# Moving the scaling of expert sums to the scalar engine, and issuing a group's token combinations closer together

## The chip, the cores and the metric

The kernel runs on one core of a Trainium2 chip. The metric is device time in microseconds (us) of one execution; lower is better. The engines are named as in the profile: PE is the TensorE matrix engine (PEld its weight loads), DVE the VectorE, ACT the ScalarE, POOL the GpSimd engine, SP the SyncE that issues most of the DMAs.

## The reference

The part that the change touches is the second half of the reference. `x` is the output of an attention stage, reordered to 2304 tokens of 512 features. `P` is a 2304 x 8 matrix of expert weights that eight rounds of row and column normalisation (Sinkhorn) make out of a softmax numerator.

```python
    logits = x @ w_gate
    P = np.exp(logits - logits.max())
    for _ in range(8):
        P /= P.sum(1, keepdims=True) + 1e-09
        P /= P.sum(0, keepdims=True) + 1e-09
        P *= N / E
    out = np.zeros((N, D), dtype=np.float32)
    for e in range(E):                       # 8 experts, every token goes through each
        h = np.maximum(x @ w1[e], 0.0)       # 512 -> 1024
        ye = h @ w2[e]                       # 1024 -> 512
        out += P[:, e:e + 1] * ye
```

## The kernel before

The attention stage fills the first 280 us or so and leaves `x` in SBUF as a high and a low part (`xh`, `xl`). Every matmul operand is split in this way, since PE multiplies rounded operands: a high part is a cast on ACT, the low part a subtraction of the high part from the full value, on POOL or DVE, and each product is three matmuls (high by high, high by low, low by high).

The expert stage works on three groups `g` of 768 tokens (6 tiles of 128, index `j`). Within a group it goes through `ITEMS`: a pair of an expert `e` and a quarter `part` of its 1024 hidden features. The first quarter of expert 0 is computed for all tokens ahead of the expert stage and stored in DRAM (`ydr`), so a group has 31 items and there are 93 in all, numbered `q` here from 0. In turn `q` the kernel computes

- the first products of item `q` (x by w1, then ReLU and the split of the result into `hhh` and `hhl`), and
- the second products of item `q - 1` (`second`, lines 868 to 884): for each `j`, six matmuls of 512 columns into one of three PSUM banks (`py`), and a DVE instruction that adds the result to the running sum `acc[:, j]`.

Most items are "fast": `first_fast` computes the first products with seven block products in place of eight by sums and differences of blocks, a Strassen-Winograd scheme (`p1, p6, p2, p7, p4, p5, p3` in this order). It needs four combinations of token blocks per group, `tcomb` (a high part `th` and a low part `tl`, index 0 to 3), which `t_tasks(g)` makes out of `xh` and `xl` in the scratch buffers `temps`. A few items are "plain" (eight block products in four pieces): items 0 to 3, and the last two of groups 0 and 1 (29, 30, 60, 61). While these run, `temps` and `tcomb` are free, and the combinations of the next group are made; the first fast item after them (4, 31 and 62) uses them from its second product on. So a fast turn has 13 pieces (7 first, 6 second), a plain one 10.

The weights of item `q + 1` are split during turn `q`: `w1_split` and `w2_split` hand out a list of jobs, one of which is issued behind each piece; casts go to ACT (`w1h`, L750 and L755, `w2h`, L778), subtractions to POOL (`w1l`, L751 and L756, `w2l`, L779).

The orders of ACT and DVE are those in which the code issues the instructions (`tc.manual_schedule`). The orders of PE, POOL and SP are set by the framework's planner when the kernel is built. Each engine runs its own list in order, with semaphores between engines.

Two things of this stage are changed. One is the scaling with expert 0's weight. For expert 0 the sums are added without a weight (L874); when expert 1 begins, ahead of the first weighted sum of each tile, DVE multiplies the running sum by expert 0's weight `P[:, t_, 0:1]` (L877), in turns 4, 35 and 66. From then on the sum is one instruction that multiplies by the weight and adds (L878). The other is the pace of `t_tasks`: twelve tasks, one in each of those pieces whose count modulo 8 is 0, 3 or 6, and one in every piece once as many tasks are left as pieces. A task `split` issues an ACT cast to `th` (L713) and the subtraction to `tl` (L710), on POOL for three of the four and on DVE for the last. The router's eight rounds (`rows`, `colmat`, `colsum`, L576 to L597) run on DVE and PE in the same turns 0 to 3 as group 0's combinations, four pieces to a round; `colmat` is a matmul into the tile `cp` that waits for `rows`.

At the end of a group the sums are stored to the output (L884) and the next group's start values are loaded from `ydr` (`acc_load`, L888), both on the queue of SP.

Of the kernel before, what the change touches and what calls it, by code (L numbers as in the profile page):

```python
# [17 lines left out]
def kernel(  # L18
# [13 lines left out]
    nc = tc.nc  # L32
# [44 lines left out]
    P = const.tile([128, NTILE, E], F32, name="P")  # L77
# [19 lines left out]
    def f32(ap):  # L97
        return ap.bitcast(F32)
# [533 lines left out]
    def product2(pt, hh, hl, w2h, w2l, cols):  # L632
        n = 0
        for f in range(2):
            for h_, w in ((hh, w2h), (hh, w2l), (hl, w2h)):
                nc.tensor.matmul(  # L636
                    out=pt, lhsT=h_[:, f, cols], rhs=w[:, f], start=(n == 0), stop=(n == 5)
                )
                n += 1
# [23 lines left out]
    HT = 384  # L663
    NG = NT // (2 * HT)

    def experts():
# [11 lines left out]
        acc = mp.tile([128, 2 * HT // 128, DM], F32, name="acc")  # L678
        tasks = router_tasks()
        tasks.reverse()  # L680

        def tick():
            if tasks:
                tasks.pop()()

        ITEMS = [
            (g, e, part) for g in range(NG) for e in range(E) for part in range(NQ)
            if (e, part) != (0, 0)
        ]
        per = E * NQ - 1  # L690
        plain = set(range(4)) | {g * per - j for g in range(1, NG) for j in (1, 2)}


        def blk(x, g, kh, th):
            c0 = (2 * g + th) * HT
            return x[:, 2 * kh:2 * kh + 2, c0:c0 + HT]

        def t_tasks(g):
            th, tl = tcomb
            s0, s1, s2 = (temps[:, i] for i in range(3))  # L700
            d, p_ = nc.vector, nc.gpsimd

            def full(o, kh, t2, eng):
                eng.tensor_tensor(
                    out=o.rearrange("p (k c) -> p k c", k=2), in0=f32(blk(xh, g, kh, t2)),
                    in1=f32(blk(xl, g, kh, t2)), op=ALU.add,
                )

            def sub(o, x, y, eng):
                eng.tensor_tensor(out=o, in0=x, in1=y, op=ALU.subtract)  # L710

            def split(i, src, eng):
                nc.scalar.copy(out=th[:, i], in_=src)  # L713
                sub(tl[:, i], src, f32(th[:, i]), eng)

            return [
                lambda: full(s0, 0, 1, d), lambda: full(s1, 0, 0, d), lambda: full(s2, 1, 1, p_),
                lambda: sub(s1, s0, s1, d), lambda: split(0, s1, p_), lambda: sub(s0, s2, s0, d),
                lambda: split(2, s0, p_), lambda: sub(s2, s2, s1, d), lambda: full(s0, 1, 0, d),
                lambda: split(1, s2, p_), lambda: sub(s0, s0, s2, d), lambda: split(3, s0, d),  # L720
            ]

        def w1_load(q):
            g, e, part = ITEMS[q]
            pool = mq if q % 2 else mp
            raws = [pool.tile([128, 512], F32, tag="raw", name="raw", bufs=2) for _ in range(2)]
            for j, raw in enumerate(raws):
                nc.sync.dma_start(
                    out=raw.rearrange("p (k f) -> p k f", k=2),
                    in_=w1[e, 256 * j:256 * j + 256, part * FQ:part * FQ + FQ]  # L730
                    .rearrange("(k p) f -> p k f", p=128),
                )
            return raws
# [9 lines left out]
        def w1_split(q, raws):  # L743
            wh, wl = w1s[q % 2]
            r0, r1 = (r.rearrange("p (k f c) -> p k f c", k=2, f=2) for r in raws)
            a11, a21, a12, a22 = r0[:, :, 0], r0[:, :, 1], r1[:, :, 0], r1[:, :, 1]
            tt = nc.gpsimd.tensor_tensor

            def one(i, src):
                nc.scalar.copy(out=wh[:, i], in_=src)  # L750
                tt(out=wl[:, i], in0=src, in1=f32(wh[:, i]), op=ALU.subtract)  # L751

            def two(i, raw):
                src = raw.rearrange("p k f c -> p f k c")
                nc.scalar.copy(out=wh[:, i:i + 2], in_=src)  # L755
                tt(out=wl[:, i:i + 2], in0=src, in1=f32(wh[:, i:i + 2]), op=ALU.subtract)  # L756


            def comb_a():
                tt(out=a22, in0=a21, in1=a22, op=ALU.add)  # L760
                tt(out=a21, in0=a11, in1=a21, op=ALU.subtract)

            def comb_b():
                tt(out=a11, in0=a22, in1=a11, op=ALU.subtract)
                tt(out=a12, in0=a12, in1=a11, op=ALU.subtract)

            if q in plain:
                return [lambda: two(1, r1), lambda: one(0, a11), lambda: one(3, a21)]
            return [
                lambda: two(1, r1), lambda: one(0, a11), comb_a, comb_b,  # L770
                lambda: two(3, r0), lambda: two(5, r1),
            ]

        def w2_split(q, raws):
            wh, wl = w2s[(q + 1) % 2]

            def one(j):
                nc.scalar.copy(out=wh[:, j], in_=raws[j])  # L778
                nc.gpsimd.tensor_tensor(  # L779
                    out=wl[:, j], in0=raws[j], in1=f32(wh[:, j]), op=ALU.subtract  # L780
                )

            return [lambda: one(0), lambda: one(1)]
# [84 lines left out]
        def second(q, j):  # L868
            g, e, part = ITEMS[q]
            t_ = 2 * HT // 128 * g + j  # L870
            pt = py[j % 3]
            product2(pt, *hs[q % 2], *w2s[(q + 1) % 2], slice(128 * j, 128 * j + 128))
            if e == 0:
                nc.vector.tensor_tensor(out=acc[:, j], in0=pt, in1=acc[:, j], op=ALU.add)  # L874
            else:
                if (e, part) == (1, 0):
                    nc.vector.tensor_scalar_mul(acc[:, j], acc[:, j], P[:, t_, 0:1])  # L877
                nc.vector.scalar_tensor_tensor(  # L878
                    out=acc[:, j], in0=pt, scalar=P[:, t_, e:e + 1], in1=acc[:, j],
                    op0=ALU.mult, op1=ALU.add,  # L880
                )
            if q % per == per - 1:
                eng = nc.scalar if g == NG - 1 and j % 2 else nc.sync
                eng.dma_start(out=out[128 * t_:128 * t_ + 128, :], in_=acc[:, j])  # L884

        def acc_load(g):
            for j in range(2 * HT // 128):
                nc.sync.dma_start(out=acc[:, j], in_=ydr[2 * HT // 128 * g + j])  # L888
# [16 lines left out]
        todo = t_tasks(0)  # L905
# [4 lines left out]
        steps, left, late = [0], [34], []  # L910
        with tc.manual_schedule(engines={mybir.EngineType.Activation, mybir.EngineType.DVE}):
            for q in range(NI + 1):
                jobs = []
                if q < NI:
                    back = w2_split(q, r2.pop(q))
                if q + 1 < NI:
                    if q + 2 < NI:
                        r1[q + 2] = w1_load(q + 2)
                    jobs = w1_split(q + 1, r1.pop(q + 1))
                    back.append(lambda q=q: r2.__setitem__(q + 1, w2_load(q + 1)))  # L920
                    jobs[4:4] = back + [lambda: None]
                elif q < NI:
                    jobs = back
                if q in plain and q + 1 in plain and q > 4:
                    todo += t_tasks(q // per + 1)
                    left[0] = 20
                pieces = (first_plain if q in plain else first_fast)(q) if q < NI else []
                if q:
                    pieces += [lambda j=j: second(q - 1, j) for j in range(2 * HT // 128)]
                for f in pieces:  # L930
                    n = len(late)
                    f()
                    for _ in range(n):
                        late.pop(0)()
                    tick()
                    if jobs:
                        jobs.pop(0)()
                    steps[0] += 1
                    if todo and (steps[0] % 8 in (0, 3, 6) or len(todo) >= left[0]):
                        todo.pop(0)()  # L940
                    left[0] -= 1
                for f in jobs:
                    f()
                if q < NI and q and q % per == 0:
                    acc_load(q // per)

    setup()
    attention()
    front.close()
    experts()  # L950


# [28 lines left out]
```

## Time and profile before

| what | value |
|---|---|
| time, three runs | 1772.06, 1772.59, 1774.39 us; median 1772.59 |
| span of the profiled execution, first to last instruction | 1770.6 us (no separate time is listed for it) |
| PE busy | 1723.7 us, 97% |
| DVE busy | 1289.0 us, 73% |
| ACT busy | 685.7 us, 39% |
| POOL busy | 1166.0 us, 66% |
| granted TensorE clock, mean | 0.996 |

A busy time is a mean over all stages; the rows further down are of single stretches. "Chain" is the chain of work that ended last, followed back from the last instruction. Matmuls overlap, so the duration of one in the trace is longer than the distance between two starts.

### The profile page before, as it was taken

How to read it: one execution, taken by the hardware profiler on the slowest of the kernel's cores; microseconds unless marked ns; L12 is line 12 of the kernel's file. 1: busy time of each engine (PE TensorE's matmuls, PEld its weight loads, DVE VectorE, ACT ScalarE, POOL GpSimd, SP SyncE). 2: the span in 40 equal slices, each digit the busy share in tenths (PEclk: the TensorE clock that was granted, in tenths of full speed). 3: DMA queues.
4: the chain of work that ended last, by engine and by line, in shares of the span. 5: the costliest groups of instructions: out<-in, count | busy, mean ns of one | idle time of the engine just before them, and what ended most of it. 6: DMA issues, size and time to landing. Idle time of an engine off the chain costs nothing.

```text
span 1770.6 us, 26969 instructions
## 1 busy us (share of the span) xinstructions
PE 1723.7 (97%) x9381; PEld 1522.5 (86%) x9381; DVE 1289.0 (73%) x2371; ACT 685.7 (39%) x1550; POOL 1166.0 (66%) x1113
## 2 busy tenths in 40 slices
PE   5899999999999999999999999999999999999999
PEld 4677777889999999888899999998898999999998
DVE  6887873787777777767777777777667777777776
ACT  4766762233333333333333333333333333333332
POOL 4655543567777777676677777776676777777773
PEclk8999999999999999999999999999999999999999
DMA  4443414222222222214222222222142222222221
GB/s 109 105 103 96 114 41 149 57 70 71 72 66 61 65 72 72 72 49 142 72 71 61 65 66 72 72 72 72 48 143 72 65 61 66 72 72 72 72 60 48
DMA packets 154888, 135.55 MB, mean 77 GB/s; under 512 B 71424, under 2 KB 121728, under 8 KB 154752
## 3 DMA queue, kind: packets, MB, share of 16 engines
q1 hardware_dynamic: 154320, 133.05, 25.0%
q8 instruction: 74, 1.21, 0.3%
q10 hardware_dynamic: 432, 0.79, 0.1%
q14 instruction: 62, 0.51, 0.1%
HBM read 124.28 MB, written 9.51 MB: 76 GB/s over the span
## 4 chain that ended last, share of the span: by engine, by line
PE 81%; POOL 5%; DVE 4%; issue 4%; DMA 2%; ACT 2%; SPq 1%; POOLq 0%; ACTq 0%; DVEq 0%
PE s L636 40%; PE s L805 27%; PE f L805 9%; PE x L470 1%; ACT e L324 1%; DMA rsb<-rd 1%; PE s L303 1%; DVE hhl L790 1%; POOL tl L710 1%; POOL phi L425 1%; POOL w1l L756 1%; DVE acc L877 0%; PE s L621 0%; PE f L636 0%; POOL w2l L779 0%
## 5 line engine op out<-in xcount | busy, mean ns | idle before, releaser
L756 POOL TENSOR_TENSOR w1l<-raw,w1h 128x512 fp32r<-128x512 f32 x263 | 368.2, 1414 | 395.1 <-ACT w1h L755 394.9
L878 DVE SCALAR_TENSOR_TENSOR acc<-s,P,acc 128x512 f32<-128x512 f32 x504 | 369.2, 745 | 133.5 <-PE s L636 131.1
L636 PE MATMUL s<-w2h,hhh 128*128 128x512 f32 x1116 | 435.5, 390 | 6.0 <-DVE acc L878 5.9
L636 PE MATMUL s<-w2h,hhl 128*128 128x512 f32 x1116 | 436.1, 391 | 0.0
L636 PE MATMUL s<-w2l,hhh 128*128 128x512 f32 x1116 | 435.8, 391 | 0.0
L836 DVE TENSOR_TENSOR temps<-s,temps 128x384 f32<-128x384 f32 x447 | 242.5, 555 | 169.8 <-ACT w1h L755 83.0
L790 DVE SCALAR_TENSOR_TENSOR hhl<-temps,hhh 128x384 fp32r<-128x384 f32 x340 | 306.5, 901 | 0.0
L779 POOL TENSOR_TENSOR w2l<-raw,w2h 128x512 fp32r<-128x512 f32 x186 | 292.7, 1595 | 11.9 <-ACT w2h L778 11.9
L789 ACT ACTIVATE hhh<-temps 128x384 fp32r<-128x384 f32 x340 | 178.7, 526 | 297.8 <-DVE temps L836 289.9
L636 PEld LDWEIGHTS s<-w2h,hhh 128*128 128x128 f32 x1116 | 209.6, 188 | 50.6 <-DVE acc L878 9.5
L636 PEld LDWEIGHTS s<-w2h,hhl 128*128 128x128 f32 x1116 | 209.4, 188 | 44.0
L636 PEld LDWEIGHTS s<-w2l,hhh 128*128 128x128 f32 x1116 | 209.4, 188 | 41.5
L839 ACT COPY temps<-s 128x384 f32<-128x384 f32 x64 | 30.7, 480 | 413.7 <-PE s L805 412.6
L805 PE MATMUL s<-th,w1l 128*128 128x384 f32 x510 | 170.8, 335 | 1.5 <-POOL w1l L756 1.5
L805 PE MATMUL s<-tl,w1h 128*128 128x384 f32 x510 | 170.7, 335 | 0.8 <-POOL tl L710 0.8
L805 PE MATMUL s<-th,w1h 128*128 128x384 f32 x510 | 170.6, 334 | 0.0
L805 PE MATMUL s<-xh,w1l 128*128 128x384 f32 x480 | 161.7, 337 | 0.5 <-POOL w1l L751 0.5
L805 PE MATMUL s<-xh,w1h 128*128 128x384 f32 x480 | 161.7, 337 | 0.0
L805 PE MATMUL s<-xl,w1h 128*128 128x384 f32 x480 | 161.2, 336 | 0.0
L755 ACT CAST w1h<-raw 128x512 fp32r<-128x512 f32 x263 | 153.7, 615 | 3.7 <-issue 3.0
L836 DVE TENSOR_TENSOR temps<-f,temps 128x384 f32<-128x384 f32 x148 | 80.3, 555 | 55.3 <-PE f L805 26.2
L778 ACT CAST w2h<-raw 128x512 fp32r<-128x512 f32 x186 | 112.1, 607 | 0.0
(220 smaller groups left out, 2895.0 us busy)
## 6 DMA issues: line engine op xcount, KB each, us to landing
raw<-in_moe_w_dram SPq DMA_DIRECT2D x372, 256.0 KB
rsb<-rd SPq DMA_DIRECT2D x32, 144.0 KB
ydr<-wst SPq DMA_DIRECT2D x18, 256.0 KB
acc<-ydr SPq DMA_DIRECT2D x18, 256.0 KB
qraw<-in_q_dram SPq DMA_DIRECT2D x32, 128.0 KB
kraw<-in_k_dram SPq DMA_DIRECT2D x32, 128.0 KB
vraw<-in_v_dram SPq DMA_DIRECT2D x32, 128.0 KB
out_dram<-acc SPq DMA_DIRECT2D x15, 256.0 KB
```

What stands on the lines that cost most here:

```text
L303: nc.tensor.matmul(out=sp[h][:, at:at + w], lhsT=qq[x][half[h], 128 * i:128 * i + 128], rhs=kk[y][half[h], 0:w], start=(a == 0), stop=(a = ...
L636: nc.tensor.matmul(out=pt, lhsT=h_[:, f, cols], rhs=w[:, f], start=(n == 0), stop=(n == 5))
L755: nc.scalar.copy(out=wh[:, i:i + 2], in_=src)
L756: tt(out=wl[:, i:i + 2], in0=src, in1=f32(wh[:, i:i + 2]), op=ALU.subtract)
L778: nc.scalar.copy(out=wh[:, j], in_=raws[j])
L779: nc.gpsimd.tensor_tensor(out=wl[:, j], in0=raws[j], in1=f32(wh[:, j]), op=ALU.subtract)
L789: nc.scalar.activation(out=hh[:, f, c], in_=src, func=AF.Relu)
L790: late.append(lambda: nc.vector.scalar_tensor_tensor(out=hl[:, f, c], in0=src, scalar=0.0, in1=f32(hh[:, f, c]), op0=ALU.max, op1=ALU.subt ...
L805: nc.tensor.matmul(out=pt[:, 0:HT], lhsT=w[:, wi, k], rhs=x[:, k], start=(n == 0), stop=(n == total - 1),)
L836: nc.vector.tensor_tensor(out=o, in0=x, in1=y, op=ALU.add)
L839: nc.scalar.copy(out=X, in_=prod(q, [(0, b11)]))
L878: nc.vector.scalar_tensor_tensor(out=acc[:, j], in0=pt, scalar=P[:, t_, e:e + 1], in1=acc[:, j], op0=ALU.mult, op1=ALU.add,)
```

## The change

Three edits, all in the expert stage. First, the multiplication by expert 0's weight becomes an ACT instruction (`acc_scale`), issued two pieces ahead of the sum that uses it; in group 0 in turn 4 as before, in groups 1 and 2 directly after the start values are loaded, in turns 32 and 63. Second, since in groups 1 and 2 the start values are now scaled ahead of expert 0's own items, these use the weighted sum (36 sums). Third, `t_tasks` becomes a list of eleven steps, some with two instructions; for groups 1 and 2 the piece count starts at 0 with the first plain turn and a step is issued in three pieces of four; the low parts 2 and 1 move from POOL to DVE, so that only low part 0 is on POOL.

```diff
+        scaled = [(0, 1, 0)] + [(g, 0, 1) for g in range(1, NG)]
...
-            def split(i, src, eng):
+            def hi(i, src):
                 nc.scalar.copy(out=th[:, i], in_=src)
+
+            def lo(i, src, eng):
                 sub(tl[:, i], src, f32(th[:, i]), eng)

             return [
-                lambda: full(s0, 0, 1, d), lambda: full(s1, 0, 0, d), lambda: full(s2, 1, 1, p_),
-                lambda: sub(s1, s0, s1, d), lambda: split(0, s1, p_), lambda: sub(s0, s2, s0, d),
-                lambda: split(2, s0, p_), lambda: sub(s2, s2, s1, d), lambda: full(s0, 1, 0, d),
-                lambda: split(1, s2, p_), lambda: sub(s0, s0, s2, d), lambda: split(3, s0, d),
+                [lambda: full(s0, 0, 1, d)],
+                [lambda: full(s1, 0, 0, d), lambda: full(s2, 1, 1, p_)],
+                [lambda: sub(s1, s0, s1, d)],
+                [lambda: sub(s0, s2, s0, d), lambda: hi(2, s0)],
+                [lambda: sub(s2, s2, s1, d), lambda: hi(1, s2)],
+                [lambda: lo(2, s0, d), lambda: hi(0, s1)],
+                [lambda: lo(1, s2, d)],
+                [lambda: full(s0, 1, 0, d), lambda: lo(0, s1, p_)],
+                [lambda: sub(s0, s0, s2, d), lambda: hi(3, s0)],
+                [lambda: None],
+                [lambda: lo(3, s0, d)],
             ]
...
-            if e == 0:
+            if e == 0 and g == 0:
                 nc.vector.tensor_tensor(out=acc[:, j], in0=pt, in1=acc[:, j], op=ALU.add)
             else:
-                if (e, part) == (1, 0):
-                    nc.vector.tensor_scalar_mul(acc[:, j], acc[:, j], P[:, t_, 0:1])
                 nc.vector.scalar_tensor_tensor(
...
+        def acc_scale(g, j):
+            t_ = 2 * HT // 128 * g + j
+            nc.scalar.mul(acc[:, j], acc[:, j], P[:, t_, 0:1])
...
                     todo += t_tasks(q // per + 1)
                     left[0] = 20
+                    steps[0] = 0
...
+                scales = []
+                if q and ITEMS[q - 1] in scaled:
+                    scales = [None] * (len(pieces) - 2 * HT // 128 - 2) + [
+                        lambda j=j: acc_scale(ITEMS[q - 1][0], j) for j in range(2 * HT // 128)
+                    ]
                 for f in pieces:
+                    if scales:
+                        s_ = scales.pop(0)
+                        if s_:
+                            s_()
...
-                    if todo and (steps[0] % 8 in (0, 3, 6) or len(todo) >= left[0]):
-                        todo.pop(0)()
+                    pace = steps[0] % 4 != 3 if q > 4 else steps[0] % 8 in (0, 3, 6)
+                    if todo and (pace or len(todo) >= left[0]):
+                        for t_ in todo.pop(0):
+                            t_()
```

## Rows read from the trace of the kernel before

**Rows 1.** The page's head: span and instructions.

```profile
span 1770.6 us, 26969 instructions
```

**Rows 2.** Chain, in order of time: start us, us, what; turns 4, 31, 35, 62 to 67.

```profile
358.89 3.14 PE s L805 x18
...
371.44 1.46 DVE acc L877
...
377.17 1.06 PE f L805 x6
...
802.91 1.06 PE s L805 x6
...
849.43 1.06 PE f L805 x6
...
867.38 1.06 PE s L805 x6
...
1291.09 2.10 PE s L805 x12
...
1298.40 8.20 PE s L636 x36
...
1313.90 8.20 PE s L636 x36
...
1337.61 1.06 PE s L805 x6
...
1355.61 2.10 PE s L805 x12
```

**Rows 3.** Timeline of PE, turns 31 and 62: start us, us, what [idle before <-releaser].

```profile
782.29 0.33 PE L805 MATMUL f<-xh,w1h 128*128 128x384 f32 x1
...
784.54 0.45 PE L805 MATMUL s<-tl,w1h 128*128 128x384 f32 x1 [0.84 <-POOL tl L710]
786.49 0.45 PE L805 MATMUL s<-th,w1l 128*128 128x384 f32 x1 [1.51 <-POOL w1l L756]
...
787.49 0.52 PE L805 MATMUL s<-xh,w1h 128*128 128x384 f32 x1
...
1272.51 0.33 PE L805 MATMUL s<-xh,w1h 128*128 128x384 f32 x1
```

**Rows 4.** Timeline of POOL, end of turn 30 and turn 31.

```profile
781.94 2.55 POOL L710 TENSOR_TENSOR tl<-temps,th 128x768 fp32r<-128x768 f32 x1
784.45 5.24 POOL L756 TENSOR_TENSOR w1l<-raw,w1h 128x512 fp32r<-128x512 f32 x3
```

**Rows 5.** Groups by line and form: xcount | busy us, mean ns | idle before <-releasers.

```profile
L878 DVE SCALAR_TENSOR_TENSOR acc<-s,P,acc 128x512 f32<-128x512 f32 x504 | 369.2, 745 | 133.5 <-PE s L636 131.1 <-DVE acc L877 0.5
...
L710 POOL TENSOR_TENSOR tl<-temps,th 128x768 fp32r<-128x768 f32 x9 | 19.6, 2181 | 4.7 <-ACT th L713 4.7
...
L877 DVE TENSOR_SCALAR acc<-acc,P 128x512 f32<-128x512 f32 x18 | 14.9, 828 | 0.0
```

**Rows 6.** Line L710 alone: duration ns min/median/max, first and last start us.

```profile
L710 DVE TENSOR_TENSOR temps<-temps x12: 948/1178/1805, 320.6 to 1274.2; 128x768 f32<-128x768 f32 x12
...
L710 DVE TENSOR_TENSOR tl<-temps,th x3: 948/1046/1052, 357.5 to 1276.4; 128x768 fp32r<-128x768 f32 x3
```

**Rows 7.** Timeline of DVE, second products in turn 29.

```profile
763.23 0.75 DVE L878 SCALAR_TENSOR_TENSOR acc<-s,P,acc 128x512 f32<-128x512 f32 x1 [0.61 <-PE s L636]
```

**Rows 8.** Timeline of DVE, router rounds in turn 2.

```profile
336.51 0.69 DVE L874 TENSOR_TENSOR acc<-s,acc 128x512 f32<-128x512 f32 x1 [0.95 <-PE s L636]
```

**Rows 9.** Groups of ACT by line and form: a cast of the sum's shape, and table loads.

```profile
L755 ACT CAST w1h<-raw 128x512 fp32r<-128x512 f32 x263 | 153.7, 615 | 3.7 <-issue 3.0 <-DMA raw<-in_moe_w_dram 0.7
...
L135 ACT ACT_TABLE_LOAD x1 | 1.3, 1283 | 0.7 <-PEq L965 0.7
```

**Rows 10.** Windows, turn 5: us, PE, PEld, DVE, ACT, POOL busy (x), PEclk, DMA, GB/s.

```profile
376.00:392.00 16.00, 16.00 (x82) 14.48 (x81) 13.15 (x21) 5.46 (x11) 11.10 (x10) 1.00 0.18 51
```

**Rows 11.** Timeline of SP: the last four loads of group 2's start values.

```profile
1295.38 4.66 SPq L888 DMA_DIRECT2D acc<-ydr  x4
```

More of the change, by code (lines that the diff above doesn't have):

```diff
@@ L929, in experts @@
                     pieces += [lambda j=j: second(q - 1, j) for j in range(2 * HT // 128)]
+                scales = []
+                if q and ITEMS[q - 1] in scaled:
+                    assert not tasks
+                    scales = [None] * (len(pieces) - 2 * HT // 128 - 2) + [
+                        lambda j=j: acc_scale(ITEMS[q - 1][0], j) for j in range(2 * HT // 128)
+                    ]
                 for f in pieces:
+                    if scales:
+                        s_ = scales.pop(0)
+                        if s_:
+                            s_()
                     n = len(late)
```

## The prediction, made before the changed kernel was run

> **What bounds the kernel now.** I read the page first: PE is busy in 97% of the span, so what can be won is time in which PE stands still, and only that. The chain of waits shows where. In the expert stage it is made of PE blocks, 18 to 36 matmuls long, and the second products of one turn begin 15.50 us after those of the turn before (1298.40 to 1313.90) [rows 2]. That is the pitch of a fast turn with PE never waiting. Five turns are longer, and they are the ones that the diff touches:
>
> - Turns 4, 35 and 66, in which DVE scales the sums, last from 358.89 to 377.17, from 849.43 to 867.38 and from 1337.61 to 1355.61 [rows 2]: 18.28, 17.95 and 18.00 us. Less 15.50 each, the loss is 2.78 + 2.45 + 2.50 = 7.73 us. The chain passes there through DVE's L877, which PE waits for because a PSUM bank is given back late [rows 2].
> - Turns 31 and 62, the first fast ones of a group, last from 782.29 [rows 3] to 802.91 [rows 2] and from 1272.51 [rows 3] to 1291.09 [rows 2]: 20.62 and 18.58 us, a loss of 5.12 + 3.08 = 8.20 us. The timeline of PE shows two waits in the second product of such a turn, first for a low part `tl`, then for weights `w1l` [rows 3]. Both come from POOL: the subtraction into `tl` starts at 781.94 and runs 2.55 us, and the three weight subtractions stand in line behind it [rows 4]. Turn 31 loses 2.04 us more than turn 62, most of it because the granted clock falls after the wait: a 384-column matmul then takes 0.52 us where it took 0.33 [rows 3], which is the lower of the two levels, 1.2 in place of 2.4 GHz. Turn 62 has the same wait and no such fall, so I count this part as one that comes and goes.
>
> In sum 15.93 us of PE standing still or slowed hang on the two things that the diff changes.
>
> **Scaling on ACT.** Removed are 18 DVE instructions of 0.828 us on average [rows 5], 14.9 us of DVE. Their cost on the path is not that but the 7.73 us above. Added are 18 ACT instructions on 128x512 float32. The trace has no scaling on ACT; the nearest row is ACT's cast of the same shape, 0.615 us [rows 9], which I take. Bounds: 0.476 us would be DVE's speed for it at best, and 0.828 its mean there [rows 5]; I use the mean as the upper end. Six cost 3.7 us (to 5.0) in a turn in which ACT is busy 5.46 of 16 us [rows 10], so ACT has room. What is queued behind a scaling on ACT: the ReLUs of `p5` and `p3`, the weight casts of the next item, then the next turn's copy. Two scalings come before the ReLU of `p3`, so it is up to 1.2 us late, but its result is used a turn later; the casts of the next weights are up to 3.7 us late, and POOL's subtractions behind them are not used until the next turn's second product. From the last sum's side: scaling 5 stands ten pieces into the turn, and its sum comes with the sixth second product, 8.20 us behind the start of the second products [rows 2]. In these 8.20 us ACT has at most four scalings and two casts, 6 x 0.615 = 3.7 us. Cost 0; without this cover a late scaling would hold DVE, and then PE, by its own length, 0.6 us each.
>
> In turns 32 and 63 the scaling waits for the start values. SP issues the last four of these loads from 1295.38 to 1300.04 [rows 11]. The second products start at 1298.40 and the last ends 8.20 us later, at 1306.6 [rows 2]. From the last issue it is 6.6 us to the sum, of which the scaling needs 0.6: the load has 6 us to land. If it lands later, ACT stands still, with the next turn's copy into `temps` behind it, which PE's second product would wait for. The 36 sums of expert 0 that now carry a weight cost what all other sums cost, 0.745 us [rows 5], against 8.20/6 = 1.37 us of PE per product [rows 2]: hidden. Credit for this edit: 7.7 us, with 5 to 7.7 as bounds.
>
> **Combinations, groups 1 and 2.** POOL loses two of its three low parts, which take 2.18 us on average [rows 5], and the third is issued at the tenth piece of the twenty, ahead of turn 30's weights. The line of POOL in front of the wait [rows 4] becomes at least 2.55 us shorter by the last low part alone, and about 4.4 us by both. The weight subtractions that started at 784.45 then start by 780 to 782, 1.75 us each (5.24/3) [rows 4], and the second product, which starts six matmuls after 782.29, finds them done or nearly so. The low part that PE waited for is now made on DVE in the ninth piece of turn 29, and the last of all, low part 3, in the fourth piece of turn 30, before that turn's six second products (8.2 us). So both waits in turns 31 and 62 go.
>
> What DVE gets for it: in the six second products of turn 29 (8.2 us) it has six sums (4.5), a late `hhl`, two differences, two low parts and a full block. With 1.05 us for a low part and 0.95 to 1.18 for a difference [rows 6] and 1.4 (estimate from these) for a full block, that is about 11 us, so DVE runs nearly 3 us late at the end. Before, it was idle 0.61 us ahead of each sum [rows 7]. PE has three banks: it needs the third sum when the sixth product starts. By then DVE has put in two differences, 2.1 us, and has gained back 3 x 0.6: the bank comes in time by about 0.8 us. The four first products of turn 30 follow with little for DVE. If the differences take 1.8 us each, the longest of their kind [rows 6], PE waits up to 0.9 us per group; I take 0.
>
> **Group 0.** Here the pace is as before, but two low parts more, 2.1 us [rows 6], fall into DVE's list between the router's rounds, and a `hi` cast now waits on ACT for a difference ahead of turn 2's first ReLU, with weight casts and POOL behind it. In turn 2 DVE still idles, 0.95 us ahead of one sum [rows 8], which takes most of a low part; the rest delays `rows`, and PE meets it at the next `cp`. Bounds: 0, if the idle time takes all, and 2.1, if none; I take 0.4, since the idle time is near the size of one low part.
>
> **Sum.** 7.7 + 8.2 - 0.4 = 15.5 us off the profiled span of 1770.6 [rows 1]. No separate time of that execution is listed; the median of the runs, 1772.59, is 2.0 above the span, and I keep that. Since one of two like turns had the slow clock and the median run may have had less of it, I count 0.5 off the gain: 1772.6 - 15.0 = 1757.6 us.
>
> **The rivals.** A change of 0.2%, 3.5 us, is about what a measurement of this kernel can tell from none.
>
> - POOL's line stays. Its order is set by the planner, not by the code. If the remaining low part is put behind turn 30's weights, or the wait at turn 31 is for the casts on ACT and not for POOL, the 8.2 us stay: 1772.6 - 7.7 + 0.4 = 1765.3. Against it: the weights' casts are done well before, and POOL is shorter in any order. 8%.
> - The scaling is late on ACT, and half or all of the 7.7 us come back as sums that wait: 1761.5 to 1765. For it speaks a rule of the Trainium skill (ScalarE: Activation LUTs, Rules for kernel authors), which gives multiplications to VectorE. The same page has 0.70 us for such an instruction (186 ns plus 0.833 ns per element plus 93 ns for the pointer operand; an estimate from What ACT_TABLE_LOAD costs); by it six would take 4.2 us in place of 3.7, and the sum would stay. Against it, from the rows: DVE's own price is 0.828 us [rows 5], it is DVE that PE waits for, and ACT is two thirds idle [rows 10]. 6%.
> - Slower: the scaling needs another function table on ACT. The trace has one table load, 1.28 us [rows 9]. Scalings, ReLUs and casts alternate, so a turn would have five visits to the other table, ten loads, 12.8 us; with 5.46 [rows 10] and 3.7 ACT would have 22.0 us of work in 15.5, and three such turns would lose 19.4 us. 1772.6 - 15.0 + 19.4 = 1777.0, slower by 0.25%. It decides from about 1.25 us per load; at 1.13 us the two cancel. Against it: copies, casts and ReLUs already share one table. 4%.
> - No change: the loss moves. DVE's crowd in turn 29 and the router's rounds take back what is won, 12 us or more, by waits that the bounds above (1.8 and 2.1 us) don't reach. 1769 to 1773. 4%.
>
> **The numbers.** My forecast, 78%, is 1757.6 us, its own range 1754.5 to 1761.5: down by group 0 at 0 and the full clock gain, up by 1.8 for turns 29 and 60 and 2.1 for group 0. To leave out no more than 2 in 10 the range reaches to the first two rivals, 1754.5 to 1765.5. Faster by over 0.2%, below 1769.0: 78 + 8 + 6 = 92%, less 2 for what I have not seen: 90%. Within 0.2%: 5%. Slower: 5%.
>
> **What would show it.** Right: the turns that begin the sums of expert 1 last 15.5 us like their neighbours; PE has no wait for `tl` or `w1l` in the first fast turn of groups 1 and 2; the granted clock stays whole there; ACT shows 18 scalings of 0.6 to 0.7 us and still one table load. Wrong: PE waiting for sums in turns 29 or 60, for `cp` in turns 2 and 3 by more than before, DVE sums that wait for ACT, a scaling that waits for its load, or POOL's low part behind the weights of turn 31.

## The result

The changed kernel takes 1758.91 us (median of four runs, 1758.08 to 1759.01) where the kernel before took 1773.49 on the same chip (four runs, 1772.06 to 1775.5): ratio 0.9914, 95% interval 0.990 to 0.9928, 14.6 us faster. Forecast were 1757.6 us and 15.0 us. The span of the profiled execution fell from 1770.6 to 1756.3 us.

The page of the changed kernel, its head and the busy time of each engine:

```profile
span 1756.3 us, 26949 instructions
...
PE 1721.0 (98%) x9381; PEld 1522.7 (87%) x9381; DVE 1280.2 (73%) x2359; ACT 695.9 (40%) x1568; POOL 1150.7 (66%) x1107
```

PE does the same 9381 matmuls; DVE, ACT and POOL barely changed. The gain is not in these shares, it is in five turns. Two of them, 4 and 31, stand in the chain of the changed kernel (start us, us, what):

```profile
359.77 3.15 PE s L815 x18
...
375.28 1.06 PE f L815 x6
...
755.81 8.38 PE s L636 x36
...
780.74 1.06 PE f L815 x6
...
796.25 1.06 PE s L815 x6
```

Turn 4 now lasts from 359.77 to 375.28 and turn 31 from 780.74 to 796.25, both 15.51 us, the pitch of a turn without waits; before they lasted over 18 and over 20 us [rows 2, 3]. The matmuls that waited in turn 31 [rows 3] now run without a gap, 0.17 to 0.18 us from start to start, in the timeline of PE:

```profile
781.64 0.33 PE L815 MATMUL s<-th,w1h 128*128 128x384 f32 x1
781.82 0.33 PE L815 MATMUL s<-tl,w1h 128*128 128x384 f32 x1
781.99 0.34 PE L815 MATMUL s<-th,w1l 128*128 128x384 f32 x1
```

Counted from the first matmul of each turn to the first of the next in both traces, the whole difference is in these places (us):

| turn | 3 | 4 | 29 | 31 | 35 | 60 | 62 | 66 | all others from 5 on |
|---|---|---|---|---|---|---|---|---|---|
| before | 18.17 | 18.29 | 16.55 | 20.46 | 17.95 | 16.55 | 18.42 | 17.99 | same |
| changed | 18.80 | 15.51 | 16.73 | 15.51 | 15.51 | 16.74 | 15.51 | 15.51 | same |

Won are 2.78 + 4.95 + 2.44 + 2.91 + 2.48 = 15.56 us, lost 0.63 + 0.18 + 0.19 = 1.00. The expert stage began 0.28 us later, though nothing ahead of it was edited, and that leaves the 14.3 us of the span. All other turns from 5 on took the same time to 0.01 us.

The instructions that were moved, and ACT's table loads, by line and form (count | busy us, mean ns | idle before):

```profile
L896 ACT ACTIVATE acc<-acc,P 128x512 f32<-128x512 f32 x18 | 12.6, 717 | 0.0
...
L711 DVE TENSOR_TENSOR tl<-temps,th 128x768 fp32r<-128x768 f32 x9 | 11.0, 1225 | 0.0
...
L711 POOL TENSOR_TENSOR tl<-temps,th 128x768 fp32r<-128x768 f32 x3 | 6.3, 2092 | 8.2 <-ACT th L714 8.2
...
L135 ACT ACT_TABLE_LOAD x1 | 1.3, 1283 | 0.7 <-PEq L990 0.7
```

A scaling takes 0.717 us on ACT, not the 0.615 that I took from the cast [rows 9], and nothing waits for it. The Trainium skill (ScalarE: Activation LUTs, What ACT_TABLE_LOAD costs) gives 0.70 us for it, an estimate by its formula for an ACT instruction with a pointer operand; the trace agrees.

### The profile page after: what moved, and what is told of

The parts are those of the page before. It is cut to its first block, busy times and chain, and to the rows that moved or that the text cites. A ratio compares the mean times of both kernels' runs of the same rounds, so it can differ in the third digit from the quotient of the medians.

```text
span 1756.3 us, 26949 instructions
## 1 busy us (share of the span) xinstructions
PE 1721.0 (98%) x9381; PEld 1522.7 (87%) x9381; DVE 1280.2 (73%) x2359; ACT 695.9 (40%) x1568; POOL 1150.7 (66%) x1107
## 4 chain that ended last, share of the span: by engine, by line
PE 88%; POOL 3%; DVE 3%; DMA 2%; issue 2%; ACT 2%; SPq 1%; POOLq 0%; ACTq 0%
PE s L636 44%; PE s L815 29%; PE f L815 10%; PE x L470 1%; ACT e L324 1%; PE s L303 1%; DVE e L317 1%; POOL phi L425 1%; DMA rsb<-rd 1%; PE s L621 0%; PE f L636 0%; POOL xc L494 0%; POOL xl L498 0%; PE x L475 0%; DMA qraw<-in_q_dram 0%
## 5 line engine op out<-in xcount | busy, mean ns | idle before, releaser
L886 DVE SCALAR_TENSOR_TENSOR acc<-s,P,acc 128x512 f32<-128x512 f32 x540 | 395.1, 744 | 146.1 <-PE s L636 146.0
```

The lines of the kernel that those rows point to most:

```text
L886: nc.vector.scalar_tensor_tensor(out=acc[:, j], in0=pt, scalar=P[:, t_, e:e + 1], in1=acc[:, j], op0=ALU.mult, op1=ALU.add,)
```

## The experiments

Each table row is one kernel. The rows were measured in three series of four, each on another chip and beside the kernel before, whose medians there were 1772.56, 1771.46 and 1772.51 us. The span is that of one profile, and with the attention stage, which no edit touches, it varies by up to 3 us; the lengths of the turns from 5 on vary far less, so the text goes by these.

| kernel | runs' median us | ratio to before, 95% interval | span us |
|---|---|---|---|
| scaling alone | 1765.33 | 0.9962, 0.9949 to 0.9975 | 1764.3 |
| combinations alone | 1766.25 | 0.9964, 0.9953 to 0.9976 | 1764.4 |
| scaling in the new place, on DVE | 1767.06 | 0.9971, 0.996 to 0.9982 | 1765.1 |
| scaling on ACT, in the old turns | 1758.15 | 0.9921, 0.9907 to 0.9936 | 1756.2 |
| new pace, low parts on POOL | 1759.32 | 0.993, 0.9913 to 0.9947 | 1758.4 |
| old pace, low parts on DVE | 1762.32 | 0.9948, 0.9933 to 0.9963 | 1759.4 |
| scaling doubled on ACT | 1757.42 | 0.9922, 0.9907 to 0.9937 | 1755.5 |
| router's step ahead of its piece | 1758.77 | 0.9928, 0.9913 to 0.9943 | 1757.0 |
| old list for group 0 | 1756.3, one run | none | 1754.5 |
| later low part in turns 1 to 3 | 1759.03, one run | none | 1757.2 |
| both of these | 1758.96 | 0.9923, 0.9909 to 0.9937 | 1757.6 |
| the changed kernel again | 1758.64 | 0.9922, 0.9909 to 0.9934 | 1756.2 |

**The two halves.** First the scaling edit with the old combinations: the cut shows the pace, and the old list of `t_tasks` and the count of pieces without its reset come with it. Then the new combinations with DVE's scaling:

```diff
-                    pace = steps[0] % 4 != 3 if q > 4 else steps[0] % 8 in (0, 3, 6)
+                    pace = steps[0] % 8 in (0, 3, 6)
```

> The scaling goes to ACT and the weighted sums of expert 0 come with it, while the token combinations keep their old list, engines and pace. My account: PE loses nothing more in the turns that begin the sums of expert 1, so the span falls by about 7.7 us to about 1763, and the first fast turn of groups 1 and 2 keeps both waits, for tl and w1l, at 2.9 us or more a turn. Rival (one cause: DVE and POOL are late together, and either edit alone would free both): the waits of the first fast turn shrink too, and the span falls by 11 us or more. Rival (the scaling is paid again on ACT): the span falls by less than 5 us.

```diff
-        scaled = [(0, 1, 0)] + [(g, 0, 1) for g in range(1, NG)]
+        scaled = []
...
+                if (e, part) == (1, 0):
+                    nc.vector.tensor_scalar_mul(acc[:, j], acc[:, j], P[:, t_, 0:1])
```

> The token combinations get the new list, engines and pace, and DVE keeps scaling the sums when expert 1 begins. My account: the two first fast turns lose nothing, group 0 pays about 0.6 us in the router's rounds, and the turns that begin expert 1 keep 18.0 to 18.3 us; the span falls by 6 to 7.6 us, to 1763 to 1764.6. With the run of the scaling alone it adds up to the whole change within 1 us. Rival (the parts overlap): the two gains add up to more than 17 us or less than 11.

The halves are independent. With the scaling alone, turns 4, 35 and 66 are 15.51 us, and turns 31 and 62 keep their waits: 20.47 and 19.92. With the combinations alone it is the other way: 15.51 for turns 31 and 62, and 17.95, 18.21 and 17.98 for the three turns of the scaling. The spans fell by 6.3 and 6.2 us, 1.8 less in sum than by the whole change, where I had expected no more than 1 us, and short of my 7.7 for the scaling. Most of it is in the windows of the run with the scaling alone: here both first fast turns fell to the lower clock, not one (columns: window, us, busy time of PE, PEld, DVE, ACT, POOL, granted clock, DMA share, GB/s):

```profile
780.50:796.00 15.50, 13.12 (x58) 11.62 (x57) 12.00 (x17) 6.29 (x12) 14.41 (x13) 0.89 0.24 77
1266.00:1281.50 15.50, 13.19 (x60) 11.91 (x60) 12.26 (x17) 6.07 (x12) 14.86 (x12) 0.89 0.16 51
```

That cost turn 62 19.92 - 18.42 = 1.50 us. In the run with the combinations alone the expert stage began 0.7 us later than in the kernel before. Windows of the changed kernel, of turn 4 and of turn 31:

```profile
359.80:375.30 15.50, 15.50 (x80) 14.06 (x79) 11.36 (x18) 8.95 (x17) 10.85 (x10) 1.00 0.19 57
780.50:796.00 15.50, 15.50 (x80) 14.06 (x79) 11.18 (x17) 5.45 (x11) 11.09 (x10) 1.00 0.28 80
```

PE is busy in the whole of both windows, the clock whole. The fall of the clock followed PE's waits for `tl` and `w1l` in three of the four turns that had them in these two profiles (the kernel before and the scaling alone). No profile without these waits has a fall between the start of the expert stage and PE's last matmul.

**Engine or place of the scaling?**

```diff
-            nc.scalar.mul(acc[:, j], acc[:, j], P[:, t_, 0:1])
+            nc.vector.tensor_scalar_mul(acc[:, j], acc[:, j], P[:, t_, 0:1])
```

> As the changed kernel, but the scaling, in its new place two pieces ahead of its sum and in turns 4, 32 and 63, is done by DVE. It tells the engine from the place. My account, that PE waits since DVE has too much to do within the second products: six more DVE instructions of 0.5 to 1.5 us fall into the same stretch, so PE waits again in each of these turns, 1 to 2.5 us, and the span is 3 to 7.5 us above the changed kernel. Rival, that the place did it (the scaling stood right ahead of the sum that needs it): the span is within 1 us of the changed kernel.

```diff
-        scaled = [(0, 1, 0)] + [(g, 0, 1) for g in range(1, NG)]
+        scaled = [(g, 1, 0) for g in range(NG)]
...
-            if e == 0 and g == 0:
+            if e == 0:
```

> As the changed kernel, but groups 1 and 2 are scaled on ACT in the turns in which expert 1 begins (35 and 66), and expert 0's sums are plain again there. My account: the turn is immaterial, ACT has room in every one and the start values are long there in both; the span is within 0.5 us of the changed kernel. Rival, that the new turn matters (the load and the scaling both early, the weighted sums): it is 1 us or more away.

It is the engine. With DVE in the new place turns 4, 32 and 63 last 18.38, 18.38 and 18.33 us, 8.6 us over 15.51 in sum, and the span is 8.8 us above the changed kernel's, more than my upper end of 7.5 for this run. In its chain, turn 32 goes through the scaling on DVE (start us, us, what):

```profile
799.07 1.06 PE s L815 x6
...
807.26 1.45 DVE acc L896
...
812.26 1.45 DVE acc L896
...
817.45 2.10 PE s L815 x12
```

and PE waits for the sums, as these waits between 800 and 820 us show (total us, times, longest):

```profile
PE s L636 <- DVE acc L886: 2.3, 2, 1.4
```

On ACT in the old turns all five turns are 15.51 us again and the span is 1756.2: neither the turn nor the weighted sums of expert 0 matter. The rule of the Trainium skill that was weighed in the prediction (ScalarE: Activation LUTs, Rules for kernel authors: multiplications to VectorE) is not borne out here, where VectorE is what the matmuls wait for: 1765.1 us of span with the scaling on DVE, 1756.3 with it on ACT.

**Is ACT's price hidden?**

```diff
             nc.scalar.mul(acc[:, j], acc[:, j], P[:, t_, 0:1])
+            nc.scalar.mul(acc[:, j], acc[:, j], ones[:, 0:1])
```

> As the changed kernel, but each scaling on ACT is followed by a second one, by ones, so its cost there is doubled to about 1.43 us per sum, 4.3 us more of ACT in each of the three turns. My account, that ACT's room hides it: the span is within 0.5 us of the changed kernel. The rival that the scaling's price on ACT is on the path: 1 to 4 us a turn, 3 us or more in all.

It is. At twice the price DVE's sums begin to wait for ACT in turn 4 (waits between 360 and 380 us; L897 is the second scaling):

```profile
DVE acc L886 <- ACT acc L897: 3.1, 4, 1.1
```

yet turn 4 stays at 15.51 us, and turns 32 and 63 are 15.57 and 15.56, 0.1 us more in all. So the 4.3 us that six more scalings take find room on ACT in such a turn; more was not tried.

**Pace or engines of the combinations?**

```diff
-                [lambda: lo(2, s0, d), lambda: hi(0, s1)],
-                [lambda: lo(1, s2, d)],
+                [lambda: lo(2, s0, p_), lambda: hi(0, s1)],
+                [lambda: lo(1, s2, p_)],
```

> As the changed kernel, with the new list and pace of the combinations, but low parts 2 and 1 are subtracted on POOL as before. It tells the pace from the engines. If the early issue in turn 29 is what removes the waits (POOL has nothing to do for some 8 us there), the first fast turns stay at 15.5 us and the span is within 0.7 us of the changed kernel. If it takes the low parts off POOL, which was the step in my prediction, POOL's line reaches into turn 31 again and the span is 2 to 6 us above it.

```diff
-                    pace = steps[0] % 4 != 3 if q > 4 else steps[0] % 8 in (0, 3, 6)
+                    pace = steps[0] % 8 in (0, 3, 6)
```

The second cut again shows only the pace; the old order of the tasks comes with it, with low parts 2 and 1 on DVE.

> As the changed kernel, but the combinations keep their old order and pace in all groups, with low parts 2 and 1 on DVE. If the engines matter most, the wait for w1l goes and that for tl shrinks: the first fast turns lose under 1 us each, and the span is at most 2 us above the changed kernel. If the pace matters most, low part 1, issued in the last pieces of turn 30, is late on DVE, where it stands behind sums and other combinations: the first fast turns lose 2 us or more each, and the span is 4 us or more above.

The new order and pace are enough by themselves. With all three low parts on POOL, issued early, turns 31 and 62 are 15.51 us, as in the changed kernel. Its span is 2.1 us longer, more than the 0.7 that I expected, but this lies elsewhere: the expert stage began 1.6 us later and turn 2 took 0.6 us more (group 0 has its low parts on POOL here too; no run shows whether that is the cause). The timeline of POOL shows why the waits are gone:

```profile
763.39 6.67 POOL L711 TENSOR_TENSOR tl<-temps,th 128x768 fp32r<-128x768 f32 x3 [1.76 <-ACT th L714]
...
779.09 2.56 POOL L766 TENSOR_TENSOR w1l<-raw,w1h 128x512 fp32r<-128x512 f32 x2
```

The three low parts, 6.67 us, begin in a stretch in which POOL waits, and the last weights are still done at 781.65, in turn 30. With the old pace and the low parts on DVE the wait for `w1l` goes, but the low parts themselves are late. PE's timeline shows the first matmul of turn 31, a stand of 0.92 us for ACT and the first matmul of turn 32, then the same first matmuls of turns 62 and 63:

```profile
778.70 0.33 PE L812 MATMUL f<-xh,w1h 128*128 128x384 f32 x1
...
784.55 0.45 PE L812 MATMUL f<-th,w1h 128*128 128x384 f32 x1 [0.92 <-ACT temps L846]
...
796.31 0.33 PE L812 MATMUL s<-xh,w1h 128*128 128x384 f32 x1
...
1264.42 0.33 PE L812 MATMUL s<-xh,w1h 128*128 128x384 f32 x1
...
1282.16 0.33 PE L812 MATMUL s<-xh,w1h 128*128 128x384 f32 x1
```

ACT's copy into `temps` waits for the last low part, which reads the same buffer, in the timeline of DVE:

```profile
782.97 0.96 DVE L711 TENSOR_TENSOR tl<-temps,th 128x768 fp32r<-128x768 f32 x1 [0.24 <-ACT th L714]
```

Turn 31 lasts 17.61 us and turn 62 17.74, so they lose 2.1 and 2.2 us, what the theory of the pace gave; turn 61 is 0.8 us longer as well. The span is only 3.1 us above the changed kernel's because the expert stage began 1.0 us earlier, turns 2 and 3 were 0.7 us shorter in sum and turns 29 and 60 0.4. With the scaling alone, which has the old pace and the low parts on POOL, there are now all four combinations. With the falls of the clock set aside, the old pace loses 5.82 us with the low parts on POOL (twice the 2.91 of turn 62 before, which had no fall) and 5.15 with them on DVE; the new one loses nothing in these turns on either engine. So a low part that is late costs on either engine.

**What is left in group 0.** Turn 3 of the changed kernel is 0.63 us longer, by PE's wait for the router's `cp`. It was 0.82 us before; in the timeline of PE it is now 1.39:

```profile
356.51 0.48 PE L585 MATMUL cp<-Pt,ones 128*128 128x144 f32 x2 [1.39 <-DVE Pt L579]
```

I tried to win it back in two ways, issuing the router's step ahead of the piece and issuing a DVE low part later:

```diff
+                    tick()
                     n = len(late)
                     f()
                     for _ in range(n):
                         late.pop(0)()
-                    tick()
```

> As the changed kernel, but a piece's step of the router is issued ahead of the piece and not behind it, so that DVE can do the column sums in the idle time ahead of the first sum of turns 1 and 3 rather than behind it. If the two remaining waits of PE for cp (0.5 us in turn 1, 1.6 us in turn 3) come from that order, they go or halve, and the span falls by 0.8 to 2 us. If they come from short DVE instructions that run longer while POOL works, the wait of turn 3 stays above 1 us and the span is within 0.7 us of the changed kernel.

```diff
+                    busy, at = bool(tasks), pieces.index(f)
                     f()
-                    for _ in range(n):
-                        late.pop(0)()
+                    if not (busy and q and at in (4, 5)):
+                        for _ in range(n):
+                            late.pop(0)()
                     tick()
+                    if busy and q and at == 5:
+                        for _ in range(n):
+                            late.pop(0)()
```

> As the changed kernel, but in turns 1 to 3 the low part of the last first product (0.55 us of DVE) is issued behind the router's next row sums and not ahead of the column sums. The low part is needed a turn later. If DVE's list between the column sums and the next row sums is what PE waits for, the waits for cp in turns 1 and 3 fall by up to 0.46 us each, from 0.5 and 1.6 to about 0.1 and 1.1. If short DVE instructions stretched by POOL set it, the turns change by under 0.2 us.

Both failed. With the router's step first, turn 3 fell to 18.49, and turn 2 rose from 17.25 to 18.42. With the later low part, DVE has 0.46 us less to do ahead of `cp`, and turn 3 is 19.05, turn 2 17.56. What took the place of the 0.46 us stands in the timelines of this kernel, DVE first, then POOL:

```profile
352.67 1.17 DVE L595 TENSOR_SCALAR cs<-cs 128x8 f32<-128x8 f32 x1
353.88 0.20 DVE L596 RECIPROCAL cs<-cs 128x8 f32<-128x8 f32 x1
354.12 1.12 DVE L597 SCALAR_TENSOR_TENSOR P<-Pt,cs 128x144 f32<-128x144 f32 x1
```

```profile
351.24 2.58 POOL L789 TENSOR_TENSOR w2l<-raw,w2h 128x512 fp32r<-128x512 f32 x2
353.78 2.59 POOL L766 TENSOR_TENSOR w1l<-raw,w1h 128x512 fp32r<-128x512 f32 x2
```

L595 adds a constant to eight columns. It ends at 353.84, when POOL's pair of subtractions ends (353.82), and took 1.17 us. In the changed kernel it begins 0.21 us earlier and ends with POOL's pair as well, 0.47 us shorter (DVE, then POOL). L577 is the same kind of instruction in the rounds' row part:

```profile
352.46 0.70 DVE L595 TENSOR_SCALAR cs<-cs 128x8 f32<-128x8 f32 x1
...
353.44 1.12 DVE L597 SCALAR_TENSOR_TENSOR P<-Pt,cs 128x144 f32<-128x144 f32 x1
...
355.40 0.33 DVE L577 TENSOR_SCALAR rs<-rs 128x18 f32<-128x18 f32 x1
```

```profile
350.57 2.57 POOL L789 TENSOR_TENSOR w2l<-raw,w2h 128x512 fp32r<-128x512 f32 x2 [0.44 <-ACT w2h L788]
353.09 2.60 POOL L766 TENSOR_TENSOR w1l<-raw,w1h 128x512 fp32r<-128x512 f32 x2
```

In the kernel before the same two are shorter, 0.26 and 0.18 us (DVE, then POOL):

```profile
352.21 0.26 DVE L595 TENSOR_SCALAR cs<-cs 128x8 f32<-128x8 f32 x1
...
354.72 0.18 DVE L577 TENSOR_SCALAR rs<-rs 128x18 f32<-128x18 f32 x1
```

```profile
351.12 2.60 POOL L779 TENSOR_TENSOR w2l<-raw,w2h 128x512 fp32r<-128x512 f32 x2
357.88 1.75 POOL L756 TENSOR_TENSOR w1l<-raw,w1h 128x512 fp32r<-128x512 f32 x1 [4.16 <-ACT w1h L755]
```

These two differences, 0.44 and 0.15 us, make 0.59 of the 0.63 us that turn 3 lost.

The old list for group 0 was the third try, alone and with the later low part:

```diff
+            if g == 0:
+                def split(i, src, eng):
+                    hi(i, src)
+                    lo(i, src, eng)
+                return [[f] for f in (...)]      # the twelve old tasks
```

> As the changed kernel, but group 0's combinations keep the old list (same pace in both, low parts 0, 2 and 1 on POOL). The changed kernel's turn 3 is 0.6 us longer than before's, with a longer wait of PE for cp. If the new list causes it, turn 3 is back at 18.1 to 18.2 us from 18.8 and the wait at 1.0 us from 1.6, and the span falls by 0.6 us, less than one look can tell by the time alone. If it is chance, turn 3 stays at 18.8.

> The old list for group 0 and the later low part together, on top of the changed kernel: turn 1 0.4 us and turn 3 1 us shorter than in the changed kernel, 1.4 us or 0.08% in all, a bound of what is left in group 0. By the rival, that POOL's work moves in and stretches what is left, under 0.5 us.

Alone it gives turn 3 back 0.57 us (18.23). The wait for `cp` is 0.83 us, and POOL is idle behind the pair of subtractions, its next instruction 4.17 us late (PE, then POOL):

```profile
354.74 0.48 PE L585 MATMUL cp<-Pt,ones 128*128 128x144 f32 x2 [0.83 <-DVE Pt L579]
```

```profile
350.16 2.60 POOL L801 TENSOR_TENSOR w2l<-raw,w2h 128x512 fp32r<-128x512 f32 x2
356.93 3.00 POOL L778 TENSOR_TENSOR w1l<-raw,w1h 128x512 fp32r<-128x512 f32 x2 [4.17 <-ACT w1h L777]
```

With the later low part as well, turn 3 is 18.46 and turn 2 18.22, and five runs gave no more than the changed kernel did beside it. The old list alone took 1756.3 us in its one run, below all five of the changed kernel on that chip (1757.56 to 1759.64). Its span is 1.7 us below that of the changed kernel's profile there: 0.9 lie ahead of the expert stage, where nothing was edited, 0.3 in turns 0 and 1 and 0.5 in turn 3; with one run and no interval, whether it beats the changed kernel stays open.

> The changed kernel once more on this chip, beside the version above: its ratio to before is 0.990 to 0.993 again, and a profile of it has no wait in the first fast turns and no fall of the clock in the expert stage. If the gain of before was partly chance, the ratio is above 0.994.

It repeated: 0.9922, the turns as in the table to 0.05 us, no wait in the first fast turns and no fall of the clock in the expert stage.

## Why the prediction was right, point by point

- The sum: 15.0 us were forecast and 14.6 measured, but the medians flatter it. The span was to fall by 15.5 us and fell by 14.3. Of the 1.2 us, 0.37 are the reading of the rows, 0.37 turns 29 and 60, 0.23 group 0 and 0.28 lie ahead of the expert stage. The medians come closer since that of before came out at 1773.49, 0.9 above the 1772.6 that I started from; that part is luck.
- My own range, 1754.5 to 1761.5, does not follow from the terms that it names: 0.4 for group 0 and the 0.5 counted for the clock lead down to 1756.7, and the upper end counts 0.4 of group 0 twice. The result lies inside either.
- The bound (PE, and five turns in which it stands still): right. All five went to the pitch; of the others from turn 5 on, all but 29 and 60 kept their length to 0.01 us. My 15.93 us was 0.37 too much, since for turns 31 and 62 I took the start from PE's timeline and the end from the chain, and for the pitch 15.50; with one kind of start it is 15.56.
- Scaling: right in the mechanism and the size, 7.70 us won of 7.73. Its price was mis-sized, 0.717 us for 0.615, and hidden, as the doubled one shows.
- The start values in turns 32 and 63: no scaling waited for its load. ACT has one table load, as before: the slower rival did not occur.
- Combinations: the size was right, 7.86 of 8.20, some 2 us of it the fall of the clock in turn 31. The step that gave the reason was wrong in part. I wrote that POOL's line becomes shorter because two low parts leave it. The run with the low parts on POOL shows that the early issue alone removes both waits, with nothing taken off POOL; taking them off without the pace wins 0.7 of 5.8 us and leaves PE waiting.
- DVE's crowd in turns 29 and 60: I took 0 with a bound of 0.9 each; it was 0.18 and 0.19. The 36 matmuls of the second products lasted 8.38 us in the chain above where those of the next turn take 8.20. It is the place that I had named: the sixth product starts at 762.55, right behind the end of DVE's third sum at 762.50. That sum is late by a difference that took 1.94 us, longer than any before (DVE, then PE):

```profile
758.37 1.94 DVE L711 TENSOR_TENSOR temps<-temps 128x768 f32<-128x768 f32 x1
```

```profile
762.55 0.50 PE L636 MATMUL s<-w2h,hhh 128*128 128x512 f32 x1
```

  That the difference was slow because POOL ran beside it is likely; no run took it apart.
- Group 0: 0.4 us was forecast and 0.63 measured, so the size was near by luck, since the step was wrong. I put it in turn 2 and counted instructions of DVE. It came in turn 3, by one of the signs that I had given for being wrong, a longer wait for `cp`: the low part ahead of POOL's weights is gone from there and ACT's casts for the next turn come earlier, so POOL's subtractions lie otherwise beside the router's short instructions, which take 0.44 and 0.15 us more. The old list brings the idle time and the shorter turn back together; that the one causes the other is argued from the ends of the instructions.
- The clock: counting 0.5 us for it was near. The profiled pair had one fall, and the granted clocks of the other runs tell the rest. Beside the experiments the kernel before ran 30 times: 15 runs have a mean clock of 0.997 and took 1771.3 us on average, twelve have 0.996 and took 1773.1, two have 0.994 and took 1775.3, and the fastest, 1769.73, has 0.998. The changed kernel's nine runs all have 0.997. So before's runs lost about 1 us to the clock on average, and their spread of 6 us, against 2 for the changed kernel, goes with it.

## What to carry to other kernels

Look for the few stretches that are longer than their neighbours, not at the busy shares: here 15.6 us sat in five turns of 93, and moving 13 us of work onto an engine that was busy 39% of the time cost nothing. When a hand-written order makes something too late for a stage boundary, issue it earlier before moving it to another engine; the early issue did all of it here, and the other engine alone 0.7 of 5.8 us. A saving of half a microsecond in front of an instruction that waits for something else can buy nothing: here L595 only waited longer.

## What the hardware showed

- Some short DVE instructions that begin while a subtraction runs on POOL end with it. L595, which adds a constant from SBUF to SBUF, took 0.17 us with POOL idle and 0.26, 0.70 and 1.17 us beside it, and ended 0.03 us behind POOL's subtraction each time. L597, which reads two SBUF operands, took 0.31 us with POOL idle and 1.12 beside it, and ended 0.17 us behind. L596 between them, a reciprocal, took 0.20 us in every case. With POOL idle, from the timeline of DVE in the kernel before:

```profile
329.58 0.17 DVE L595 TENSOR_SCALAR cs<-cs 128x8 f32<-128x8 f32 x1
...
330.02 0.31 DVE L597 SCALAR_TENSOR_TENSOR P<-Pt,cs 128x144 f32<-128x144 f32 x1
```

  The Trainium skill (SBUF — State Buffer, Who interferes with whom) says that DVE's second port pair is shared with GpSimd as an exclusive lock for a whole instruction, and that a `tensor_scalar` in a 2-port mode and instructions with two SBUF inputs contend for it. The traces agree; that L595 runs in such a mode is not shown.
- The same waits of PE, 0.8 and 1.5 us in a turn that lost 2.9 by them, were followed by a fall to half clock, 0.52 in place of 0.33 us for a 384-column matmul, in one of two turns in one execution and in both in another, at about 1.5 to 2 us each. No run shows what decides it.
